# Reordered small-matmul bursts of an attention layer inside a matmul-bound MLP kernel

## The chip, the cores and the metric

The kernel runs on one core of one Trainium2 chip. The metric is the device time of one execution in microseconds (us). Three runs of the kernel before the change took 314.78, 314.87 and 315.19 us; the median is 314.87 us. Below, TensorE is PE, VectorE is DVE, ScalarE is ACT, GpSimd is POOL and SyncE is SP.

## What is computed

Two layers follow each other. The first is an "hourglass" attention over q, k, v of shape 8 batches x 8 heads x 576 positions x 64:

```python
q_d, k_d, v_d = means over 4 neighbouring positions      # 144 positions
out_d = softmax(q_d k_d^T / 8) v_d, each row repeated 4 times
scores = where(|i - j| < 4, q k^T / 8, -1e9)             # a narrow band
out = out_d + softmax(scores) v
```

The second is an MLP on x, the attention output as 4608 tokens x 512: `h = x @ w_in` (512 x 2048), `g = h * sigmoid(1.702 h)`, `y = g @ w_out` (2048 x 512). Inputs and output are fp32; the matmuls run in bf16.

## The kernel before

**Two streams on one engine.** The 4608 tokens are cut into 9 groups of 512. For each group, `mm1` makes h in 16 chunks of 128 columns (4 matmuls of 128x512 each, L764), ACT turns each chunk into gT (Silu, L775), and `mm2` multiplies gT by w_out (64 matmuls of 128x512, L845, 16 for each of four blocks of 128 tokens); ACT scales each result and SP stores it (L828). The attention of batch b = g + 1 is computed while the MLP works on group g. PE executes its instructions in the order in which the program writes them, and that order is written by hand: each group's matmuls are counted, and at the counts in `POS = [12, 16, 33, 41, 53]` (for group 0 `POS_0`) a step of the attention is put in. So batch 1 is computed in group 0, batches 2 to 7 in groups 1 to 6; groups 7 and 8 have no attention, and batch 0 is computed ahead of everything by code of its own.

**The steps of one batch** are these. Heads come in two halves, qd = 0 and qd = 1.

- Count 12 (inside `mm1`): the score burst of qd = 0, `scores_mixed`, on PE. It writes three PSUM tiles: `P[0]` gets the pooled (144-column) scores, `P[1]` and `P[2]` get the band's scores. `P` is PA[0..2] from batch 2 on, and a rotation of the same three tiles in batch 1.
- Count 16 (end of `mm1`): ACT loads the exponential's table and reads the qd = 0 scores out of PSUM: `exp_local` of `P[1]`, then of `P[2]` (L446), and last `exp_down` of `P[0]` (L461). DVE multiplies the band's results by a mask (L469).
- Count 33 (17 matmuls into `mm2`): the score burst of qd = 1, into the same three PSUM tiles, and then ACT's reads, now `exp_down` first and the band's two after it.
- Counts 41 and 53: the AV bursts `avx(b, (0, 1))` and `avx(b, (2, 3))` (batches 2 to 7), into PA[0] and PA[2] (the "mains") and PA[1] (the "rest"). ACT and DVE then normalise and write xT, which the next group's `mm1` reads. Batch 1 has four smaller bursts of another function, `avx1`.

**The score burst** has 104 matmuls: 24 of `scores_d` (L435; 6 rounds of 4, each 32 rows x 144 columns), and 80 of `local` (L408; 20 rounds of 4, each 32 rows x 60 columns). Ten `local` rounds are of "half 1", and are written in turn with the six rounds of `scores_d` (the mixed rounds); the ten of "half 0" stand by themselves. In the qd = 0 burst the mixed rounds come first and the half-0 rounds last. In the qd = 1 burst the half-0 rounds come first.

**The AV burst** `avx` has 88 matmuls in 22 rounds of 4, each round on the four 64x64 quarters of the array: six rounds `down` of 144 columns (L632), and 16 rounds `local` (L654): five `main` and four `rest` (57 or 60 columns), two `extra` and one denominator of 60, two denominators of 114 into the mains, and two (`rest_den`) of 114 into PA[1]. Before, the six `down` rounds come first, then `main` and denominators in turn, then `rest`.

What PE waits for is set by the tile framework from the data: a matmul waits for the last reader of the PSUM tile that it overwrites, and for the writers of its operands.

Of the kernel before, what the change touches and what calls it, by code (L numbers as in the profile page):

```python
# [19 lines left out]
def kernel(  # L20
# [380 lines left out]
    def scores_mixed(b, qd, P):  # L401
        def local(i, a, half):
            for r in range(4):
                par = half if r < 2 else 1 - half
                rows = slice(32 * r, 32 * r + 32)
                k0 = 114 * i + KSTART[par]
                q0 = 114 * i + QSTART[par]
                nc.tensor.matmul(  # L408
                    P[1 + r // 2][64 * par : 64 * par + 64, r % 2, 60 * i : 60 * i + 60],
                    lhsT=kT[b, qd][rows, k0 : k0 + 64, a],  # L410
                    rhs=qT[b, qd][rows, q0 : q0 + 60, a],
                    start=(a == 0), stop=(a == 1),
                    tile_position=(32 * r, 64 * par),
                )

        if qd:
            for n in range(10):
                local(n // 2, n % 2, 0)
        for n in range(6):
            scores_d(b, qd, P[0], (n,))  # L420
            for a in range(2 if n < 5 else 0):
                local(n, a, 1)
        if not qd:
            for n in range(10):
                local(n // 2, n % 2, 0)
        return P[0], P[1:3]

    def scores_d(b, qd, sd=None, rounds=range(6)):
        bank = [sd[:, u, :] for u in range(2)]
        for n in rounds:  # L430
            kc, a = n // 2, n % 2
            for r in range(4):
                rows = slice(32 * r, 32 * r + 32)
                u, j = (r // 2, r % 2) if b < 1 else (r % 2, r // 2)
                nc.tensor.matmul(  # L435
                    bank[u][64 * j : 64 * j + 64, SD * kc : SD * kc + SD],
                    lhsT=kdT[qd][rows, 48 * kc : 48 * kc + 64, a],
                    rhs=qdT[b, qd][rows, :, a],
                    start=(a == 0), stop=(a == 1),
                    tile_position=(32 * r, 64 * j),  # L440
                )
        return sd
# [97 lines left out]
    def sub(t, off, *dims):  # L540
        return bass.AP(
            tensor=t.tensor, offset=t.offset + off,
            ap=[list(t.ap[0])] + [list(d) for d in dims],
        )
# [77 lines left out]
    def avx(b, hps):  # L622
        vb, vd = vbs[b % 2], vds[b % 2]

        def mains(par):
            return PA[2 * par]

        def down(kc, den):
            for u, hp in enumerate(hps):
                rows = slice(64 * u, 64 * u + 48)  # L630
                for j in range(2):
                    nc.tensor.matmul(  # L632
                        mains(u)[64 * j : 64 * j + 64, den, DN : DN + SD],
                        lhsT=ones[rows, 1, :] if den else vd[rows, kc, hp // 2 * 2 + j, 0:D],
                        rhs=eds[hp // 2][rows, j, SD * kc : SD * kc + SD],
                        start=(kc == 0), stop=(kc == 2),
                        tile_position=(64 * u, 64 * j),
                    )

        def local(den, to, what):  # L640
            for par in range(2):
                hp = hps[par] if to == "main" else hps[1 - par]
                i, c0, ni, n = what[par]
                rows = slice(64 * par, 64 * par + 64)
                if to == "rest":
                    t, bk = PA[1], par
                    at = 256 * den + 57 * (i - 1 + par)
                else:
                    t, bk = mains(par), den
                    at = 57 * i + c0 if par == 0 else 57 * i  # L650
                    if to == "extra":
                        at = EX
                for j in range(2):
                    nc.tensor.matmul(  # L654
                        t[64 * j : 64 * j + 64, bk, at : at + ni * n],
                        lhsT=ones[rows, 0, :] if den else vb[rows, i, 2 * hp + j, 0:D],
                        rhs=sub(es[hp][rows, j, :], 60 * i + c0, (60, ni), (1, n)),
                        start=True, stop=True,
                        tile_position=(64 * par, 64 * j),
                    )  # L660

        def rest(k):
            local(0, "rest", ((k + 1, 3, 1, 57), (k, 0, 1, 57)))

        def rest_den(k):
            local(1, "rest", ((k + 1, 3, 2, 57), (k, 0, 2, 57)))

        def main(k):
            local(0, "main", ((k, 3 if k else 0, 1, 57 if k else 60),
                              (k, 0, 1, 57 if k < 4 else 60)))  # L670

        def extra(den):
            local(den, "extra", ((0, 0, 1, 60), (4, 0, 1, 60)))

        for kc in range(3):
            down(kc, 0)
            down(kc, 1)
        main(0)
        local(1, "main", ((1, 3, 2, 57), (0, 0, 2, 57)))
        main(1)  # L680
        local(1, "main", ((3, 3, 2, 57), (2, 0, 2, 57)))
        main(2)
        local(1, "main", ((0, 0, 1, 60), (4, 0, 1, 60)))
        main(3)
        extra(0)
        main(4)
        extra(1)
        for k in range(4):
            rest(k)
            if k % 2 == 0:  # L690
                rest_den(k)

        l = work.tile([128, 2, S + SD], FP32, name="l", tag="l", bufs=2)
        n = work.tile([128, 2, S + SD], FP32, name="n", tag="n", bufs=1)
# [40 lines left out]
    def attention(b):  # L735
        st = {}

        def s_pe(qd):
            P = PB if b == 1 else PA
            st["d", qd], st["s", qd] = scores_mixed(b, qd, P)  # L740

        def s_act(qd):
            if qd == 0:
                nc.scalar.preload_act_table_set("natural_log_exp_and_others")
            if qd:
                exp_down(qd, st["d", qd])
            exp_local(qd, st["s", qd], (1, 0) if qd else (0, 1))
            if not qd:
                exp_down(qd, st["d", qd])
            mask_local(qd)  # L750

        def s1():
            s_pe(1)
            s_act(1)

        first = [lambda: s_pe(0), lambda: s_act(0), s1]
        if b == 1:
            return first + [lambda hp=hp: avx1(b, hp) for hp in range(HP)]
        return first + [lambda: avx(b, (0, 1)), lambda: avx(b, (2, 3))]
# [282 lines left out]
```

## Time and profile before

| what | value |
|---|---|
| median of three runs | 314.87 us |
| the profiled execution: its own time | 315.19 us |
| its span in the trace | 313.4 us |
| PE busy | 305.3 us, 97% of the span |
| ACT busy | 208.5 us, 67% |
| POOL, DVE busy | 152.0 us (49%), 146.3 us (47%) |
| granted PE clock | full in every slice of the span |
| start-to-start of two groups' score bursts (134.86 to 167.33 us) | 32.47 us |

The span is the time between the first and last instruction on record; the 1.8 us between it and the execution's own time lie outside the trace's instructions. In the timeline view each row gives the start and the length in us, the engine, the line, the shapes and the number of instructions merged into it. A matmul's length on record includes its way through the array (379 ns for a 128x512 one), while the next one starts 216 ns later; so starts, not lengths, tell what a matmul costs.

### The profile page before, as it was taken

The page shows a single profiled execution, that of the slowest core. Times are in us where ns is not written, and L with a number is a line of the kernel's source. Part 1 is how long each engine was busy: PE and PEld are TensorE (multiplying, and loading weights), DVE is VectorE, ACT ScalarE, POOL GpSimd, SP SyncE. Part 2 cuts the span into 40 slices and gives each one's busy share as a digit, 9 for nine tenths or more (in the row PEclk, how much of TensorE's full clock was granted, in tenths as well). Part 3 has the DMA queues.
Part 4 walks back from the last instruction along what each step waited for, and adds up shares of the span by engine and source line. Part 5 has one row for each costly group of instructions (what it writes and reads, how often), then busy time and mean ns, then how long its engine had stood idle before and what let it go on. Part 6 is the DMA issues. An engine that isn't in the chain of part 4 may idle for free.

```text
span 313.4 us, 9902 instructions
## 1 busy us (share of the span) xinstructions
PE 305.3 (97%) x4308; PEld 161.6 (52%) x4308; DVE 146.3 (47%) x302; ACT 208.5 (67%) x332; POOL 152.0 (49%) x174
## 2 busy tenths in 40 slices
PE   7799999999999999999999999999999999999995
PEld 3468657644644555455545554555455544444444
DVE  7972926761495059604980399028912760000000
ACT  8685775787867687668865895588568857316611
POOL 8852393295238943795359734983397210000000
PEclk9999999999999999999999999999999999999999
DMA  7999999999727951697159814991330110011011
GB/s 118 127 202 210 178 113 207 213 245 227 143 94 181 204 130 69 159 221 164 38 184 203 186 37 148 195 201 67 122 102 29 43 69 0 33 67 36 0 67 67
DMA packets 64123, 39.96 MB, mean 128 GB/s; under 512 B 44624, under 2 KB 54992, under 8 KB 64080
## 3 DMA queue, kind: packets, MB, share of 16 engines
q0 software_dynamic: 18864, 14.95, 34.1%
q1 hardware_dynamic: 45072, 24.32, 29.7%
q8 instruction: 33, 0.54, 0.7%
q14 instruction: 10, 0.08, 0.1%
q10 hardware_dynamic: 144, 0.07, 0.1%
HBM read 44.83 MB, written 9.44 MB: 173 GB/s over the span
## 4 chain that ended last, share of the span: by engine, by line
PE 93%; POOL 2%; DMA 2%; ACT 1%; issue 1%; DVE 0%; POOLq 0%; ACTq 0%
PE pm L845 37%; PE pm L764 25%; PE pa L764 15%; PE pa L408 3%; PE pa L845 2%; PE pa L654 2%; PE pa L435 2%; PE pa L632 2%; DMA vb<-in_v_dram 2%; PE pm L860 1%; POOL vb L232 1%; PE pa L567 1%; PE pa L474 1%; PE pa L525 0%; PE pa L555 0%
## 5 line engine op out<-in xcount | busy, mean ns | idle before, releaser
L845 PE MATMUL pm<-w_out_bf,gT 128*128 128x512 bf16 (+1 forms) x550 | 119.5, 371 | 0.0
L764 PEld LDWEIGHTS <-w_in_bf 128*128 128x128 bf16 x614 | 59.4, 98 | 62.5 <-issue 0.3
L764 PE MATMUL pm<-xT,w_in_bf 128*128 128x512 bf16 (+1 forms) x366 | 89.0, 371 | 0.1
L845 PEld LDWEIGHTS <-gT 128*128 128x128 bf16 x604 | 57.0, 98 | 59.6 <-issue 0.8
L775 ACT ACTIVATE gT<-pm 128x512 bf16<-128x512 f32 x88 | 52.7, 603 | 41.0 <-PE pm L764 41.0
L764 PE MATMUL pa<-xT,w_in_bf 128*128 128x512 bf16 (+1 forms) x248 | 59.0, 358 | 0.0
L469 DVE TENSOR_TENSOR es<-es,mask 128x600 bf16<-128x600 bf16 x28 | 16.3, 616 | 88.7 <-ACT es L446 88.5
L828 ACT ACTIVATE osb<-pm 128x512 f32<-128x512 f32 (+2 forms) x35 | 20.3, 582 | 30.5 <-PE pm L845 28.0
L724 POOL TENSOR_TENSOR xT<-xT,od 128x576 bf16<-128x576 bf16 x12 | 17.6, 1471 | 38.8 <-DVE xT L708 38.3
L775 ACT ACTIVATE gT<-pa 128x512 bf16<-128x512 f32 x56 | 32.1, 609 | 6.4 <-PE pa L764 6.3
L708 DVE TENSOR_TENSOR xT<-n,l 128x285 bf16<-128x285 f32 (+1 forms) x96 | 28.2, 370 | 0.0
L310 POOL TENSOR_TENSOR pq<-kT 128x576 f32<-128x576 bf16 x11 | 12.7, 1159 | 30.4 <-DVE kT L279 30.4
L830 DVE TENSOR_SCALAR osb<-pm 128x128 f32<-128x128 f32 x1 | 0.3, 291 | 54.0 <-ACT osb L828 54.0
L327 POOL TENSOR_TENSOR pq<-v 112x512 f32<-112x512 f32 x18 | 23.8, 1321 | 3.0 <-DMA v<-in_v_dram 2.9
L279 DVE STREAM_TRANSPOSE kT<-kb 128x576 f32<-128x576 f32 x16 | 20.0, 1249 | 3.0 <-DMA kb<-in_k_dram 3.0
L232 POOL DMA_DIRECT2D vb<-in_v_dram x20 | 13.7, 697 | 14.6 <-DMA w_in_bf<-in_moe_w_in_dram 4.6
L279 DVE STREAM_TRANSPOSE qT<-qb 128x576 f32<-128x576 f32 x16 | 19.9, 1243 | 0.2 <-DMA qb<-in_q_dram 0.2
L461 ACT ACTIVATE ed<-pa 128x864 bf16<-128x864 f32 x16 | 14.3, 894 | 4.9 <-PE pa L435 4.9
L446 ACT ACTIVATE es<-pa 128x600 bf16<-128x600 f32 x28 | 17.2, 669 | 0.1
L703 ACT ACTIVATE l<-l 128x1440 f32<-128x1440 f32 x12 | 16.8, 1404 | 0.4
L697 ACT ACTIVATE l<-pa 128x492 f32<-128x492 f32 x24 | 12.6, 578 | 6.0 <-PE pa L654 6.0
L698 DVE COPY n<-pa 128x492 f32<-128x492 f32 x24 | 15.0, 665 | 2.8 <-ACT l L697 2.2
(120 smaller groups left out, 363.0 us busy)
## 6 DMA issues: line engine op xcount, KB each, us to landing
out_dram<-osb SPq DMA_DIRECT2D x34, 256.0 KB, 2.1
vf<-in_v_dram SPq DMA_DIRECT2D x60, 128.0 KB, 4.4
v<-in_v_dram SPq DMA_DIRECT2D x72, 96.0 KB, 3.1
kb<-in_k_dram POOLq DMA_DIRECT2D x16, 288.0 KB, 6.6
qb<-in_q_dram POOLq DMA_DIRECT2D x16, 288.0 KB, 8.3
w_out_bf<-in_moe_w_out_dram POOLq DMA_DIRECT2D x4, 512.0 KB, 13.9
vb<-in_v_dram POOLq DMA_DIRECT2D x20, 64.0 KB, 5.5
w_in_bf<-in_moe_w_in_dram POOLq DMA_DIRECT2D x2, 512.0 KB, 7.9
```

Of the source, the lines that this page charges most:

```text
L232: nc.gpsimd.dma_start(out=vbs[b % 2][64 * par : 64 * par + 64, i, :, 0:D], in_=bass.AP(tensor=v.tensor, offset=v[b, 0].offset + (114 * i + ...
L279: nc.vector.transpose(out=t32.rearrange("p (i c) -> p c i", c=18), in_=store[b, qd].bitcast(FP32).rearrange("p (c d) -> p c d", c=18),)
L327: eng.tensor_tensor(out=t1[0:112], in0=x[:, :, 0:2, :], in1=x[:, :, 2:4, :], op=ALU.add)
L446: nc.scalar.activation(out=es[2 * qd + u][:, :, 0:300], in_=sp[u][:, :, 0:300], func=AF.Exp, scale=inv_sqrt_d,)
L469: nc.vector.tensor_tensor(out=ev, in0=ev, in1=mask, op=ALU.mult)
L703: nc.scalar.activation(out=l, in_=l, func=AF.Exp, scale=-1.0)
L708: nc.vector.tensor_tensor(out=out, in0=sub(n, *part), in1=sub(l, *part), op=ALU.mult)
L724: eng.tensor_tensor(out=xs, in0=xs, in1=sub(od[:, u, :], 0, (1, SD), (0, 4)), op=ALU.add)
L764: nc.tensor.matmul(acc[:, c : c + n], lhsT=w_in_bf[:, dmc, ffc * 128 : (ffc + 1) * 128], rhs=xT[dmc][:, g * TG + c : g * TG + c + n], star ...
L775: nc.scalar.activation(out=gT[:, ffc, :], in_=acc, func=AF.Silu, scale=GELU_SCALE)
L828: eng.activation(out=osb, in_=ap, func=AF.Copy, scale=1.0 / GELU_SCALE)
L845: nc.tensor.matmul(ops[t][:, c : c + wide], lhsT=gT[:, ffc, t * 128 : (t + 1) * 128], rhs=w_out_bf[:, ffc, c : c + wide], start=(ffc == 0) ...
```

## The change

Two functions are edited. In `scores_mixed` the qd = 1 burst takes the order of the qd = 0 burst: mixed rounds first, then the ten half-0 rounds. In `avx` (batches 2 to 7) the 22 rounds are put in another order: the five `main` and one `extra` first, then `down`, denominators, `extra` and `rest` interleaved, with both `rest_den` last. No instruction is added or removed on any engine; ACT, DVE, POOL and SP keep their order, and the steps stay at their counts.

```diff
@@ scores_mixed @@
-        if qd:
-            for n in range(10):
-                local(n // 2, n % 2, 0)
         for n in range(6):
             scores_d(b, qd, P[0], (n,))
             for a in range(2 if n < 5 else 0):
                 local(n, a, 1)
-        if not qd:
-            for n in range(10):
-                local(n // 2, n % 2, 0)
+        for n in range(10):
+            local(n // 2, n % 2, 0)
@@ avx @@
-        for kc in range(3):
-            down(kc, 0)
-            down(kc, 1)
-        main(0)
-        local(1, "main", ((1, 3, 2, 57), (0, 0, 2, 57)))
-        main(1)
-        local(1, "main", ((3, 3, 2, 57), (2, 0, 2, 57)))
-        main(2)
-        local(1, "main", ((0, 0, 1, 60), (4, 0, 1, 60)))
-        main(3)
+        def den(*what):
+            local(1, "main", what)
+
+        for k in range(5):
+            main(k)
         extra(0)
-        main(4)
+        down(0, 0)
+        down(1, 0)
+        den((1, 3, 2, 57), (0, 0, 2, 57))
         extra(1)
-        for k in range(4):
-            rest(k)
-            if k % 2 == 0:
-                rest_den(k)
+        down(2, 0)
+        den((0, 0, 1, 60), (4, 0, 1, 60))
+        down(0, 1)
+        rest(0)
+        down(1, 1)
+        rest(1)
+        down(2, 1)
+        rest(2)
+        den((3, 3, 2, 57), (2, 0, 2, 57))
+        rest(3)
+        rest_den(0)
+        rest_den(2)
```

## The prediction

> **What bounds the kernel now.** I read the page first: the busy shares and the chain that ended last.
>
> ```profile
> PE 305.3 (97%) x4308; PEld 161.6 (52%) x4308; DVE 146.3 (47%) x302; ACT 208.5 (67%) x332; POOL 152.0 (49%) x174
> ...
> PE 93%; POOL 2%; DMA 2%; ACT 1%; issue 1%; DVE 0%; POOLq 0%; ACTq 0%
> ```
>
> PE is busy almost throughout and makes 93% of the chain. From batch 2 on, a group has 128 big matmuls at 0.216 us (the chain shows 64 of L845 in 13.81 us), 27.62 us, and four bursts; between the big matmul's start before a burst and the one's after it lie 1.35 us (first score burst), 1.52 (second) and 2 x 1.40 (AV), less 0.216 each: 4.80. The sum, 32.42, is the group's 32.47 us. So nothing but PE's own sequence counts, and what a burst grows by goes to the end.
>
> Next, PE's timeline at both score bursts of one batch (start, length, engine, line, shape, count). The first burst, mixed rounds first:
>
> ```profile
> 134.86 0.26 PE L435 MATMUL pa<-qdT,kdT 32*64 32x144 bf16 x4
> ...
> 135.46 0.51 PE L408 MATMUL pa<-qT,kT 32*64 32x60 bf16 x40
> 135.90 1.47 PE L764 MATMUL pm<-xT,w_in_bf 128*128 128x512 bf16 x6
> ```
>
> and the second, half-0 rounds first:
>
> ```profile
> 142.60 0.59 PE L845 MATMUL pm<-w_out_bf,gT 128*128 128x512 bf16 x2
> 143.13 0.51 PE L408 MATMUL pa<-qT,kT 32*64 32x60 bf16 x40
> 143.64 0.26 PE L435 MATMUL pa<-qdT,kdT 32*64 32x144 bf16 x4
> ...
> 144.34 1.90 PE L845 MATMUL pm<-w_out_bf,gT 128*128 128x512 bf16 x8
> ```
>
> From its first small matmul to the next big one the first takes 135.90 - 134.86 = 1.04 us, the second 144.34 - 143.13 = 1.21. The extra lies at one place: the 40 half-0 matmuls start within 0.32 us (about 0.032 a round), yet L435 starts only at 143.64, some 0.17 us after it could have. Why, ACT's timeline tells:
>
> ```profile
> 140.18 1.28 ACT L744 ACT_TABLE_LOAD   x1
> 141.48 1.23 ACT L446 ACTIVATE es<-pa 128x600 bf16<-128x600 f32 x2
> 142.59 0.90 ACT L461 ACTIVATE ed<-pa 128x864 bf16<-128x864 f32 x1
> 143.37 0.62 ACT L828 ACTIVATE osb<-pm 128x512 f32<-128x512 f32 x1
> 144.59 0.89 ACT L461 ACTIVATE ed<-pa 128x864 bf16<-128x864 f32 x1 [0.61 <-PE pa L435]
> ```
>
> ACT frees PSUM in the order band, band, pooled: the pooled scores of qd = 0, in `P[0]`, are read last, until 142.59 + 0.90 = 143.49. The second burst's L435 writes that very tile. It starts 0.14 us after this end, and so in each later batch (batch 3: 110.87 to 111.02; 5: 175.96 to 176.10; 6: 208.43 to 208.58; 7: 240.89 to 241.04; in batch 2 78.41 to 78.46). The half-0 rounds need only the two tiles that ACT frees 0.8 us earlier: today they fill the wait.
>
> **Score bursts, part by part.** Nothing is added or removed; the order of 104 matmuls changes. On PE a waiting matmul holds all behind it: first the 40 half-0 matmuls, then the 8 big ones up to the AV burst. ACT's part is the same instructions behind the same last matmul of `mm1`, so the end at 143.49 stays, and L435, now first, still starts at 143.64. Behind it the burst runs as the first one does, 1.04 us: the next big matmul starts at 144.68 instead of 144.34, **0.34 us later**. That is the half-0 rounds' own time, no longer under the wait. By batch: 4 to 7 have 0.70 to 0.71 from L435 to the big matmul, so 4 x 0.34 = 1.36. Batch 2 has 79.26 - 78.46 = 0.80, batch 3 has 111.87 - 111.02 = 0.85; their last L435s came 0.08 and 0.15 late, for a reason the trace doesn't show. If that stays they lose 0.34 each, if not 0.25 and 0.19; I take the middle, 0.56 for both. **Sum 1.92 us.**
>
> Does it come back? `exp_down` of qd = 1 waits for the last L435, which comes 0.54 us after the first in the first burst and 0.53 in the second: no earlier. PSUM is free for the AV burst at 146.05 (mains) and 146.61 (PA[1]), and that burst now starts at 146.51, its first `rest` some 0.57 later: no wait. DVE and ACT behind the AV bursts move with PE; next group's xT keeps its 0.6 us in hand. Could the wait go faster with nothing before it? Its lag, 0.05 us in batches 1 and 2 and 0.14 in the others, bounds that: -0.09 x 5 to +0.09.
>
> **Batch 1 is another case.**
>
> ```profile
> 42.86 1.04 PE L845 MATMUL pm<-w_out_bf,gT 128*128 128x512 bf16 x7
> 44.28 1.02 PE L845 MATMUL pa<-w_out_bf,gT 128*128 128x512 bf16 x4 [0.38 <-ACT ed L461]
> ```
>
> Its pooled read ends at 42.10, and L435 starts at 42.16, right after the half-0 rounds. Mixed first, L435 stays there and the big matmuls come at 43.20 instead of 42.86. But after eight halves (0.11 each, done at 43.74 now and 44.08 then) PE stops until 44.28 for ACT's `exp_down` of qd = 1, which waits for the same last L435. The 0.34 vanishes in this stop: **0**; at most 0.34, if `exp_down` came 0.34 later.
>
> **AV bursts, 12 of them.** Same 22 rounds. From the rows of one burst (146.17 to 147.26), by single rounds:
>
> ```profile
> 146.44 0.23 PE L632 MATMUL pa<-ed,vd 48*64 48x144 bf16 x4
> 146.51 0.23 PE L632 MATMUL pa<-ed,ones 48*64 48x144 bf16 x4
> 146.57 0.20 PE L654 MATMUL pa<-es,vb 64*64 64x60 bf16 x4
> 146.60 0.22 PE L654 MATMUL pa<-es,ones 64*64 64x114 bf16 x4
> 146.66 0.20 PE L654 MATMUL pa<-es,vb 64*64 64x57 bf16 x4
> ```
>
> a 144-column round costs 0.062, a 114-column one 0.054, a short one 0.031; the first one 0.09 if long, and 0.053 if short (the half-0 start). Before: 0.09 + 5 x 0.062 + 4 x 0.054 + 11 x 0.031 = 0.957 to the last round, then 0.13 to the big matmul. After: 0.053 + 11 x 0.031 + 6 x 0.062 + 3 x 0.054 = 0.928, and the exit behind a 114-column round 0.13 + 57 columns x 0.42 ns = 0.155. 1.083 against 1.087 us: **nothing**. The hope of long and short in turn is that a long round covers a short one's weight load. In the rows a short round after a long one takes 0.027 to 0.031, after a short one 0.030 to 0.033, while 114 columns beside short ones cost 0.054 where streaming needs 0.048: what one gains the other returns. Bounds: if every round went at its columns alone (0.42 ns each) a burst would gain 0.13; if the front of short rounds drained PE's queue (as in the first score burst, where some 0.1 passes without a start once about 35 matmuls have gone out) it would lose 0.1. I take 0, as in the plain sum.
>
> **Sum:** the profiled execution took 315.19 us, 1.8 of it outside its span of 313.4. 315.19 + 1.92 = 317.11. It was the slowest of the three shown; against the median, 314.87 + 1.92 = **316.8 us**. About 0.2% (0.6 us) is what a measurement of this kernel tells from no change.
>
> **Rivals.**
> - *The wait is the price of waiting inside a burst, not a wait for ACT.* Then mixed-first costs 1.35, as the first burst does, instead of 1.52 (1.665 in batch 3): -0.17 x 5 - 0.31 = -1.15, 313.7 us, **faster**. For it: five bursts take the same 1.52. Against: L435 follows ACT's end by 0.14 even in batch 3, where both come later, and both use the same tile. It decides if `exp_down` ended before about 143.0. Chance 0.04.
> - *Covered weight loads.* Up to -0.13 x 12 = -1.5 on top of the forecast; half of it gives 316.0, all 315.2. Chance 0.07.
> - *An empty queue in the AV bursts:* +0.1 x 12: 318.0. Against: the half-0 start sends out 40 matmuls in short rounds without a hole. Chance 0.05.
> - *Drains between shapes.* `down` uses 48 rows of a quarter, `local` 64; the new order switches ten times a burst, the old once. The nearest price is the entry from a 128-row matmul: 143.13 - 142.82 = 0.31 where 0.216 is usual, so 0.093 a switch, 9 x 12 x 0.093 = +10, 327 us. Against: the one switch in the rows above, 146.51 to 146.57, costs a plain 0.062, and batch 1's `avx1` mixes both shapes without holes of that size. Chance 0.02. The Trainium skill, "TensorEngine Tiling (Array Packing)", section Key Properties, states that a change of tiling mode drains TensorE; by that, an order with ten switches would be this rival if 48 and 64 rows were different modes. The trace's one switch says they are not.
> - *The change is absorbed as in batch 1*, by a stop I overlooked: 314.9. The 32.42 of 32.47 us leaves no room. Chance 0.03.
>
> **How the numbers follow.** The forecast has 0.79. Its own parts: scores +1.3 to +2.5, AV bursts within 0.03 each, 0.36 in all, so 316.2 to 317.7; it also takes in the weak half of covered loads and stops short of the queue. Range 316.0 to 317.9. Slower has the forecast, the queue, the drains and most of the covered loads: 0.92; same 0.04; faster 0.04.
>
> **What would show it.** Right: in the second bursts L435 comes first, 0.14 us after the end of ACT's pooled read (0.05 in batch 2), at the same distance from `mm1`'s end as now; 1.04 us later the big matmul; big to big about 1.86 us instead of 1.52; batch 1's stop down from 0.38 to about 0.05; AV bursts at 1.40 still; groups 32.8 us apart. Wrong: a second burst of 1.35, L435 before ACT's end, AV bursts away from 1.40 by over 0.03, or a new stop at the AV bursts' start.

## The result, and the profile after

The changed kernel takes **317.85 us** (317.17 to 318.16, 6 runs), the kernel before, on the same chip, 315.25 us (314.78 to 315.67, 6 runs): a ratio of 1.0079, interval 1.0062 to 1.0096. By the ratio that is 2.5 us more (interval 2.0 to 3.0; 2.6 between the medians); the forecast was 1.9 more, 316.8 us, with a range up to 317.9.

The profiled execution took 318.10 us, its span is 316.3. Its page lacks 42 of PE's 4308 matmul records, 22 of them the first big matmul behind a burst; every weight load is on record. So the ends of bursts are taken here from weight loads (the next big matmul's first one), in both kernels. For the same reason the chain that ended last is not usable: with its steps missing it wanders off PE.

```profile
PE 299.6 (95%) x4266; PEld 161.3 (51%) x4308; DVE 146.5 (46%) x302; ACT 208.6 (66%) x332; POOL 149.7 (47%) x174
...
PE 51%; POOL 17%; issue 10%; DMA 8%; ACT 7%; DVE 6%; SPq 0%; POOLq 0%; DVEq 0%
```

PE's timeline at the second score burst of batch 4, the one shown before; `scores_d` is now L431, `mm2` L846:

```profile
143.74 0.59 PE L846 MATMUL pm<-w_out_bf,gT 128*128 128x512 bf16 x2
144.77 0.26 PE L431 MATMUL pa<-qdT,kdT 32*64 32x144 bf16 x4 [0.44 <-POOL vd L330]
...
145.36 0.65 PE L408 MATMUL pa<-qT,kT 32*64 32x60 bf16 x40
146.17 1.67 PE L846 MATMUL pm<-w_out_bf,gT 128*128 128x512 bf16 x7 [0.16 <-issue]
```

and ACT's:

```profile
142.61 1.23 ACT L442 ACTIVATE es<-pa 128x600 bf16<-128x600 f32 x2
143.73 0.90 ACT L457 ACTIVATE ed<-pa 128x864 bf16<-128x864 f32 x1
144.50 0.62 ACT L829 ACTIVATE osb<-pm 128x512 f32<-128x512 f32 x1
145.72 0.89 ACT L457 ACTIVATE ed<-pa 128x864 bf16<-128x864 f32 x1 [0.61 <-PE pa L431]
```

The burst begins with L431, and not before 144.77, 0.14 us behind the end of ACT's pooled read. PE has nothing before it: the stretch from the last big matmul is idle. The view names POOL as the releaser, but in the profiles of four kernels (before, changed, e1, e7) `scores_d` started, from batch 3 on, 20 to 243 ns behind that POOL instruction, and 143 to 146 ns behind ACT's read (50 to 57 in batches 1 and 2): it is ACT.

Where the time went, between the first score burst of batch 1 and the end (275.31 us before, 277.58 after: +2.27; the other 0.68 of the two spans' difference lies ahead of it, where nothing was changed, and the start varied between 37.7 and 39.0 us over all these profiles):

| place | before | after | us in all |
|---|---|---|---|
| second score bursts, batches 2 to 7 (end of first to end of second burst) | 8.44 (8.58 in batch 3) | 8.68, 8.77, 8.91, 8.92, 8.87, 8.77 | +2.15 |
| AV bursts, 12 | 1.084 each | 1.098 each | +0.17 |
| batch 1, second burst and the stretch behind it | 3.745 + 26.923 | 4.081 + 26.555 | -0.03 |

### The profile page after: what moved, and what is told of

Its sections match the earlier page's. It is cut to its first block, busy times and chain, and to the rows that moved or that the text cites. A ratio compares the mean times of both kernels' runs of the same rounds, so it can differ in the third digit from the quotient of the medians.

```text
span 316.3 us, 9861 instructions
## 1 busy us (share of the span) xinstructions
PE 299.6 (95%) x4266; PEld 161.3 (51%) x4308; DVE 146.5 (46%) x302; ACT 208.6 (66%) x332; POOL 149.7 (47%) x174
## 4 chain that ended last, share of the span: by engine, by line
PE 51%; POOL 17%; issue 10%; DMA 8%; ACT 7%; DVE 6%; SPq 0%; POOLq 0%; DVEq 0%
PE pm L846 18%; PE pm L765 13%; PE pa L765 9%; DMA vf<-in_v_dram 5%; POOL pq L310 4%; DVE xT L709 4%; POOL vb L320 3%; PE pa L846 2%; POOL pq L327 2%; DMA vb<-in_v_dram 2%; PE pa L408 2%; ACT l L704 2%; PE pa L650 2%; POOL xT L725 2%; POOL vb L232 2%
## 5 line engine op out<-in xcount | busy, mean ns | idle before, releaser
L846 PE MATMUL pm<-w_out_bf,gT 128*128 128x512 bf16 (+1 forms) x527 | 115.0, 370 | 3.2 <-issue 3.0
L765 PE MATMUL pm<-xT,w_in_bf 128*128 128x512 bf16 (+1 forms) x351 | 87.0, 371 | 0.5
L846 PEld LDWEIGHTS <-gT 128*128 128x128 bf16 x604 | 57.0, 98 | 59.3 <-issue 0.4
L725 POOL TENSOR_TENSOR xT<-xT,od 128x576 bf16<-128x576 bf16 x12 | 15.4, 1281 | 43.3 <-DVE xT L709 43.3
```

Source lines behind the costliest of these rows:

```text
L725: eng.tensor_tensor(out=xs, in0=xs, in1=sub(od[:, u, :], 0, (1, SD), (0, 4)), op=ALU.add)
L765: nc.tensor.matmul(acc[:, c : c + n], lhsT=w_in_bf[:, dmc, ffc * 128 : (ffc + 1) * 128], rhs=xT[dmc][:, g * TG + c : g * TG + c + n], star ...
L846: nc.tensor.matmul(ops[t][:, c : c + wide], lhsT=gT[:, ffc, t * 128 : (t + 1) * 128], rhs=w_out_bf[:, ffc, c : c + wide], start=(ffc == 0) ...
```

## The experiments

In the table, "bursts" is the sum over batches 2 to 7 of the time from the end of the first score burst to the end of the second, less that of the kernel before (50.77 us), and less 0.216 for each big matmul that was moved ahead of it. "Elsewhere" is what else changed in every batch; what batches 1 and 2 lose beside that is left out, because it differs from profile to profile, with edits that don't touch these batches too (0.9 us in e4's, 1.7 in e5's, 0.2 in e6's, 0.9 in e9's, 2.3 in e10's, 0.7 in e11's). The ratios stand against runs of the kernel before on the same chip; e7 and e11 ran once and have none.

| run | bursts, us | elsewhere, us | ratio (interval) |
|---|---|---|---|
| e1 scores alone | +2.25 | 0 | 1.0066 (1.0041 to 1.0090) |
| e2 AV alone | -0.08 | AV +0.17 | 1.0015 (0.9991 to 1.0039) |
| e3 mixed first, 3 later | -0.77 | next group +1.0 | 1.0016 (1.0001 to 1.0032) |
| e4 old order, 1 later | -0.66 | 0 | 0.9976 (0.9962 to 0.9989) |
| e5 pooled read first | +1.15 | 0 | 1.0034 (1.0014 to 1.0054) |
| e6 fifteen ahead | -0.64 | 0 | 0.9983 (0.9963 to 1.0003) |
| e7 changed, no v loads for 4 to 7 | +1.88 | AV +0.17 | one run, 316.73 us |
| e8 mixed first 3 later, AV 2 later | -0.69 | 0 | 0.9977 (0.9960 to 0.9995) |
| e9 e6 with v early | -0.83 | next group +5.7 | 1.0187 (1.0143 to 1.0230) |
| e10 changed with v early | +2.01 | AV +0.17, next group +6.0 | 1.0304 (1.0271 to 1.0337) |
| e11 AV without turns | -0.11 | AV +0.13 | one run, 315.54 us (before: 315.32) |

**The two parts alone.** e1 takes the hunk of `scores_mixed`, e2 that of `avx`.

> Only the second score burst is put mixed-first; the AV bursts stay as before. Theory (the burst's front now waits for ACT's read of the pooled scores, with nothing before it): second bursts of batches 2 to 7 end about 2.1 us later in all than before, AV bursts stay at 1.084 us, batch 1 gains nothing and loses nothing; total +2.0 us, between +1.7 and +2.4. Rival (the AV order carries a good part of the +2.6): +1.3 or less.

> Only the AV bursts take the new order. Theory: each of the 12 bursts goes from 1.084 to 1.098 us, from its first weight load to the next big matmul's; total +0.17 us, which is below what the timing can tell from no change. Second score bursts stay at 1.21. Rival (AV order costs more than its own bursts, through later logs and a later xT): +0.5 or more.

e1 has all of the loss, and AV bursts of 1.085. e2's AV bursts take 1.098 and nothing behind them grows: the stretches from burst to burst and to the next group stay within 0.003 us. Both rivals fall, e2's by the profile alone: its ratio's interval is too wide to tell +0.17 us from +0.5.

**Mixed first without a wait.**

```diff
-    POS = [12, 16, 33, 41, 53]
+    POS = [12, 16, 36, 44, 53]
```

> Scores mixed-first as in the change, AV order as before, but the second score burst stands three big matmuls later (count 36) and the first AV burst as well (44). Three big matmuls are 0.65 us; the wait in front of the burst is 0.60. Theory: the wait is gone, the burst takes 1.04 us as the first one does, the total is 0.17 us a batch below before, -0.8 to -1.2 us (about 314). Rival (mixed-first costs by itself): still +1.5 or more above before.

The first part came as the theory has it: L431 follows the big matmuls without a wait and the bursts gain 0.77 us. So mixed-first costs nothing by itself. But the time didn't fall: 0.15 to 0.18 us a batch is lost again behind the AV bursts. PE's timeline of e3 at the next group's `mm1` (now L760), and DVE's:

```profile
157.28 0.60 PE L760 MATMUL pm<-xT,w_in_bf 128*128 128x512 bf16 x2
157.72 0.59 PE L760 MATMUL pa<-xT,w_in_bf 128*128 128x512 bf16 x2
158.31 0.38 PE L760 MATMUL pm<-xT,w_in_bf 128*128 128x512 bf16 x1
```

```profile
157.50 1.42 DVE L720 TENSOR_TENSOR xT<-xT,od 128x576 bf16<-128x576 bf16 x2
```

The two matmuls from 157.72 leave PE free at 158.15; the next one reads the third part of xT, which the first of DVE's two instructions finishes at about 158.2. DVE runs without a pause from the AV bursts to here, and the first AV burst had been moved three matmuls towards it. e8 puts that burst one matmul back:

```diff
-    POS = [12, 16, 36, 44, 53]
+    POS = [12, 16, 36, 43, 53]
```

> Mixed-first three big matmuls later as in the run before, but the first AV burst only two later (count 43, not 44). There the bursts had gained 0.77 us and PE lost 0.16 us a batch at the next group's matmuls, which waited for DVE's last xT. Theory: with 0.216 us more for DVE this wait is gone and the gain stays: -0.6 to -0.9 us against before. Rival (the loss behind the AV bursts has another cause): +0.2, as in that run.

```profile
158.35 0.59 PE L760 MATMUL pa<-xT,w_in_bf 128*128 128x512 bf16 x2
158.79 0.38 PE L760 MATMUL pm<-xT,w_in_bf 128*128 128x512 bf16 x1
```

158.79 - 158.35 = 0.44, two matmuls and no gap: the new wait is gone, and the gain stays, -0.69 us.

**The wait of the old order.** e4 keeps both old orders and moves the steps by one big matmul.

```diff
-    POS = [12, 16, 33, 41, 53]
+    POS = [12, 16, 34, 42, 53]
```

> Both orders as before; the second score burst one big matmul later (count 34), the AV bursts too (42 and 54). One big matmul is 0.216 us, the wait inside the burst about 0.19. Theory: that wait is gone, the burst takes 1.04 us instead of 1.21: -0.8 to -1.2 us, the same time as mixed-first three later. Rival (the 0.17 is the price of a wait inside a burst): no change.

(The kernel that ran has 53 as its last count, not 54 as the expectation says: the second AV burst stayed.) PE's timeline and ACT's:

```profile
143.98 0.52 PE L408 MATMUL pa<-qT,kT 32*64 32x60 bf16 x40
144.36 0.26 PE L435 MATMUL pa<-qdT,kdT 32*64 32x144 bf16 x4
```

```profile
143.23 0.90 ACT L461 ACTIVATE ed<-pa 128x864 bf16<-128x864 f32 x1
```

L435 starts 0.23 us behind the end of ACT's read (144.13), so it no longer waits for it. Bursts that had no hole (see below) take 1.08 to 1.09 instead of 1.21: 0.12 of the 0.17 was a wait for ACT and no price of waiting. Some 0.04 stays, with no wait for ACT left: L435 starts 0.38 behind the burst's first matmul in batches 3 to 7, and 0.345 in batch 2. So the gain, 0.66 us in the bursts, falls short of the 0.8 to 1.2 expected.

e6 leaves the counts and puts more work under the wait:

```diff
         if qd:
             for n in range(10):
                 local(n // 2, n % 2, 0)
-        for n in range(6):
-            scores_d(b, qd, P[0], (n,))
-            for a in range(2 if n < 5 else 0):
-                local(n, a, 1)
+            for n in range(5):
+                local(n // 2, n % 2, 1)
+            for n in range(6):
+                scores_d(b, qd, P[0], (n,))
+                if n < 5:
+                    local((n + 5) // 2, (n + 5) % 2, 1)
         ...  # the first burst, qd = 0, keeps its order
```

> Order of before, but in the second score burst 15 band rounds stand ahead of the first pooled round (ten of half 0, five of half 1), and only five are mixed with the pooled ones; counts as before. 15 rounds are 0.49 us, the wait ends 0.51 after the burst's start. Theory: almost no wait is left, the burst takes 1.04 to 1.10 us instead of 1.21: -0.7 to -1.0 us against before. Rival (rounds out of the mix cost more than the wait gave): no change or slower.

```profile
142.65 0.67 PE L408 MATMUL pa<-qT,kT 32*64 32x60 bf16 x60
143.20 0.26 PE L441 MATMUL pa<-qdT,kdT 32*64 32x144 bf16 x4
```

Sixty short matmuls, then L441 0.55 us after the start: three bursts take 1.08, three 1.16 (with holes, below). The sum is -0.64 us, a little less than expected. In this profile the first AV burst of batch 2 also waited 0.27 us for POOL's pooled v.

**The order of ACT's reads.** e5 is e1 with

```diff
-            if qd:
-                exp_down(qd, st["d", qd])
+            exp_down(qd, st["d", qd])
             exp_local(qd, st["s", qd], (1, 0) if qd else (0, 1))
-            if not qd:
-                exp_down(qd, st["d", qd])
```

> Second score burst mixed-first, AV order as before, and ACT reads the pooled scores of qd = 0 first, the band's two tiles after it. If the wait for the pooled tile alone made the loss, L435's front would be free 1.2 us earlier and the burst would start as before: -0.8 us against before. Theory: the mixed rounds write all three tiles within their first eight matmuls, so the wait moves to the band's matmuls and ends with ACT's last read, which stays at the same time: the same time as mixed-first alone, +2.0 us (+1.7 to +2.4).

```profile
144.61 0.26 PE L431 MATMUL pa<-qdT,kdT 32*64 32x144 bf16 x4
144.62 0.21 PE L408 MATMUL pa<-qT,kT 32*64 32x60 bf16 x2
145.02 0.22 PE L408 MATMUL pa<-qT,kT 32*64 32x60 bf16 x4 [0.16 <-ACT es L442]
```

```profile
142.96 0.89 ACT L457 ACTIVATE ed<-pa 128x864 bf16<-128x864 f32 x1
143.75 1.23 ACT L442 ACTIVATE es<-pa 128x600 bf16<-128x600 f32 x2
```

L431 starts at once, and the third band matmul waits for ACT's last read, until 143.75 + 1.23 = 144.98. The wait moved to the tile that is now read last, as expected, but the loss is 1.15 us and not 2.0: six matmuls are out of the way, and this wait ends 0.04 us behind ACT's read where L431's ends 0.14 behind.

**The holes.** A hole is a pause inside a burst, beyond the two that every mixed burst has (last section), that no wait in the trace accounts for. Some second bursts take more than 1.03 us from their first matmul: 1.13 to 1.19 in batches 4 to 6 of the changed kernel, and in the kernel before batches 2 and 3 have one. In all 13 profiles batch 7, which loads nothing more, has none. SP's queue in the kernel before issues the next batch's v through the whole burst (143.13 to 144.34):

```profile
135.73 9.07 SPq L221 DMA_DIRECT2D vf<-in_v_dram  x10
```

> The changed kernel without the loads of v for batches 4 to 7 (the band's products there use batch 3's values). In the changed kernel some second bursts of batches 3 to 6 take 0.10 to 0.16 us more than 1.03 from their first matmul, batch 7 never. If these holes come from the v transfers that run then, batches 3 to 6 take 1.03 to 1.04 each; if not, one or more of the four still shows a hole of over 0.05.

Batches 3 to 6 take 1.034 to 1.036, batch 2, whose next load is still there, 1.147. So, as far as this one profile and the batches 7 go, the second bursts have holes only where these transfers run. They are not enough by themselves: batches 4 to 6 of the kernel before have them and no hole. What in them stops PE isn't shown. The first score bursts take 1.04 without a hole under as much traffic (219 GB/s at 136 to 137 us, against 176 at 144.7 to 145.9, in the changed kernel).

e9 and e10 tried to move the transfers out of the burst, in a kernel that computes everything:

```diff
             prep_qk(b, 0)
+            prep_v(b, nc.gpsimd)
+            if b + 1 < B:
+                load_v(b + 1)
             pool_qk(b, 0)
             if b + 1 < B:
                 for qd in range(NQ):
                     load_qk(b + 1, qd)
-            prep_v(b, nc.gpsimd)
-            if b + 1 < B:
-                load_v(b + 1)
```

> The fifteen-ahead order, and POOL converts v before it pools q and k, so that the next batch's v loads, which wait for this, are issued some 3 us earlier by SP (now from 135.7 to 144.8 us in one group, through the second score burst). Theory (holes come from v transfers): issues end before the burst; if the issues matter the bursts take 1.08 each with no holes and the total is -0.8 to -1.0 us against before; if the packets in flight matter (they land 4 us after their issue) holes stay in some and the total is as without the edit, about -0.6. Rival: q and k are pooled 2.4 us later and the first score burst waits: slower by more than 0.5.

> The changed kernel with the same edit of POOL's order. With issues as the cause of the holes: second bursts of 1.03 to 1.04 us from their first matmul in all batches, total +2.0 to +2.1 against before; with packets in flight as the cause: holes of 0.05 to 0.16 in some batches as in the changed kernel.

Neither answers: the loads were issued from 134.15 us to 146.8 in e9, through the second burst still, and holes stayed in two batches of each. In both the first score bursts of batches 2 to 6 ran while v was being issued, too: batch 2's got a hole of 0.14 us, the other eight took 1.04 without one. Both lost 1.1 to 1.2 us a batch at another place. PE's, POOL's and DVE's timelines of e9:

```profile
128.51 0.38 PE L770 MATMUL pm<-xT,w_in_bf 128*128 128x512 bf16 x1 [0.96 <-DVE xT L730]
```

```profile
123.41 2.32 POOL L320 CAST vb<-vf 128x2560 bf16<-128x2560 f32 x1
```

```profile
123.98 2.06 DVE L714 TENSOR_TENSOR od<-n,l 128x288 f32<-128x288 f32 x1
```

The same DVE product takes 0.45 us in e6. Beside POOL's conversion it takes 2.06 and ends 0.3 us behind it; this is in DVE's chain to xT, and PE waits for it. The rival "q and k are pooled later" expected a loss of this size at another place, the first score burst; a wait for POOL's qdT stands there only in batch 2 of e10 (0.45 us).

**AV rounds without the turns.** e11 keeps the new front and end of `avx`, with pooled rounds, denominators and rests each in a block.

```diff
         for k in range(5):
             main(k)
         extra(0)
-        ...  # the rounds in turn
+        for kc in range(3):
+            down(kc, 0)
+            down(kc, 1)
+        local(1, "main", ((1, 3, 2, 57), (0, 0, 2, 57)))
+        local(1, "main", ((3, 3, 2, 57), (2, 0, 2, 57)))
+        local(1, "main", ((0, 0, 1, 60), (4, 0, 1, 60)))
+        extra(1)
+        for k in range(4):
+            rest(k)
         rest_den(0)
         rest_den(2)
```

> Scores as before; the AV bursts begin with the same six short rounds and end with the same two 114-column rounds as in the change, but long and short rounds are not in turn: the six pooled rounds stand together, the denominators together, the rests together. If the turns are what made the changed bursts 0.014 us longer (1.098 against 1.084), these take 1.08; if the short front or the long end did, they take 1.098.

1.095 us: 0.003 less than with turns. So of the 0.014, 0.011 is there with the new front and end alone, and only the rest comes with the turns.

## Why the prediction was right, point by point

The mechanism held, but the time stood only 0.05 us inside the range, and that is partly luck. The forecast's own terms reached to 317.7, not to 317.85. The time lies 1.05 us above the 316.8 forecast; 0.38 of that is the kernel before itself, whose six runs have a median that much above the three from which the forecast started. Of the 0.6 us between the forecast and the measured difference 0.23 stands in the score bursts and 0.17 in the AV bursts; the rest lies within the interval.

- **The bound.** Right. Every microsecond that a burst gained or lost stood in the total, except where a stop behind it took it (batch 1, e3).
- **L435 first, and held by ACT's pooled read.** Right to 0.01 us: 7.735 to 7.737 us after the end of the first burst in batches 3 to 7, where L435 stood at 7.736 to 7.738 before. e3, e4 and e8 remove the wait in three ways and the loss turns into a gain of 0.66 to 0.77 in the bursts; e1 shows the whole loss in it. The rival "price of a wait" is refuted by e4, though of the 0.17 us that the prediction read as this wait 0.04 is none.
- **1.04 us behind it.** Right in batches 2, 3 and 7 (1.03 to 1.04). In batches 4 to 6 it is the mis-sized term: 1.13 to 1.19, because the holes, which the prediction met in batches 2 and 3 only and took for half, turned up there. Batches 4 to 7 were put at 1.36 us and cost 1.72, batches 2 and 3 at 0.56 and cost 0.43; together 2.15 instead of 1.92. They move from run to run (the e1 profile has them in batches 3 to 6), so no sum from one profile could place them.
- **Does it come back?** Right: from the second burst's end to the AV burst 1.83 us before and after, no new wait.
- **Batch 1: 0.** Right: -0.03. The burst ends 0.34 us later and PE's stop for `exp_down` takes it.

```profile
44.10 0.82 PE L846 MATMUL pm<-w_out_bf,gT 128*128 128x256 bf16 x6 [0.16 <-issue]
44.95 1.02 PE L846 MATMUL pa<-w_out_bf,gT 128*128 128x512 bf16 x4
```

The halves end at 44.92, the stop is 0.03 where it was 0.38.

- **AV bursts: nothing.** The step that failed, by a little: 1.098 instead of 1.083, +0.17 us in all. The exit was right (0.152 from the last round to the big matmul, 0.155 forecast); from the first round to the last it takes 0.945 where the sum has 0.928. The mis-sized term is the six pooled rounds, 0.390 instead of 6 x 0.062 = 0.372; the other rounds cost what was forecast. A pooled round and the short one behind it cost 0.096 here, where the prices added to 0.093:

```profile
148.30 0.24 PE L628 MATMUL pa<-ed,ones 48*64 48x144 bf16 x4
148.36 0.20 PE L650 MATMUL pa<-es,vb 64*64 64x57 bf16 x4
148.39 0.24 PE L628 MATMUL pa<-ed,ones 48*64 48x144 bf16 x4
148.46 0.20 PE L650 MATMUL pa<-es,vb 64*64 64x57 bf16 x4
148.49 0.24 PE L628 MATMUL pa<-ed,ones 48*64 48x144 bf16 x4
```

In e11 five of the pooled rounds stand behind one another and the six cost 0.378, but the short rounds cost 0.007 more; why is open. The same rows refute the drains: these switches between 48 and 64 rows cost 0.003 a pair, not 0.093 each. The rule weighed there (the Trainium skill, "TensorEngine Tiling (Array Packing)", Key Properties) speaks of a drain when the tiling mode changes; by these rows 48 and 64 rows of the same quarters are no such change.

Three versions beat the kernel before by the same small amount: e4 and e8 by 0.24 and 0.23% with intervals clear of 1 (e8's barely), e6 by 0.17% with one that touches it.

## What to carry to other kernels

When a burst reuses buffers that another engine frees one by one, order its work as they are freed, and put what needs the last one behind as much as it takes to cover the wait; an order that is good where nothing is awaited can lose where something is. Before moving a step of a full engine, look at what runs without a pause behind it: in e3 the gain of one wait came back as another at DVE's end. And a term that moves between batches without a known reason is a range, not a mean.

## What the runs showed of the hardware

- In a burst that begins with the mixed rounds 32 packed matmuls start within 0.18 us; then comes a pause of 0.10 us (0.07 in the changed kernel's second bursts, behind their wait), another of 0.065 after 64, and from the first pause on one starts every 8 to 9 ns. So a score burst of 104 takes 1.04 us mixed first, once it may start; with the half-0 rounds first it took 1.04 in batch 1 and 1.08 to 1.09 in e4's later bursts without a hole.
- Some second score bursts get holes of 0.03 to 0.15 us while v is being loaded, and none of e7's did without.
- DVE's fp32 product of two SBUF operands took 2.06 us beside a POOL conversion and 0.45 without. The Trainium skill, "SBUF — State Buffer", section "SBUF: two separate sides", says that DVE operations with two SBUF inputs and GpSimd operations that read SBUF exclude each other for a whole instruction; the trace agrees, the product ending 0.31 us behind the conversion.
- A matmul released by ACT starts 0.05 us behind the read's end in batches 1 and 2, and 0.14 from batch 3 on. There the wait for ACT stands in a sequencer instruction of its own (EVENT_SEMAPHORE, 0.05 us) ahead of the weight load, which also waits for POOL; in batch 2 the weight load had gone ahead and the matmul alone waited.
